# Twelve blocks of tokens in place of thirteen, in a gated scan followed by two MLPs on one core

## The chip, the core and the metric

The kernel runs on one core of a Trainium2 chip. TensorE (PE in the profile) does the matrix products, VectorE (DVE) and ScalarE (ACT) the elementwise work, SyncE (SP) issues most DMAs. The metric is the time of the device in microseconds, lower is better. A run of the kernel before takes 1091.85 us (median of three, 1091.34 to 1092.14).

## The reference

There are 6080 tokens of 256 channels. A gated scan runs along the tokens, channel by channel, and its output goes through two MLPs with 2048 hidden units each, one after the other:

```python
sig = 1.0 / (1.0 + np.exp(-f_logit))
f = lower_bound + (1.0 - lower_bound) * sig
i = 1.0 - f
for t in range(S):
    h = f[:, t] * h + i[:, t] * x[:, t]
    y[:, t] = h

h = y @ w_in_1                                  # 256 -> 2048
y1 = (h * sigmoid(1.702 * h)) @ w_out_1         # 2048 -> 256
h = y1 @ w_in_2
g = where(h >= 1, h, where(h <= -1, 0, (h + 1) ** 2 / 4))
out = g @ w_out_2
```

Inputs, `lower_bound` and the output are float32, the four weight matrices float64.

## The kernel before, in words

Channels and hidden units lie on the 128 partitions, tokens along the free axis. `token_blocks` cuts the 6080 tokens, 190 units of 32, into the fewest blocks of at most `MAXN` tokens, as even as units allow, the longer ones first. With `MAXN = 480` these are 8 blocks of 480 and then 5 of 448. A block goes through layer one and later through layer two.

A float32 operand of a product is split into a high and a low part of type float32r, and a product takes three matmuls: high by high, high by low, low by high (`three`, lines 298 to 300). A step is two tiles of 128 hidden units of one block in one layer: `up` makes the hidden values (two halves of the channels, two tiles, three passes: 12 matmuls), the activation follows on ScalarE and VectorE, `high` and `low` split it, and `down`, two steps later, adds the product with the output weights to the block's result (12 matmuls). A block takes 8 steps in each layer. A matmul has 128 x 128 stationary weights, and as many columns as the block has tokens; the weights change with every matmul.

The order of the steps: the first three blocks go through layer one together, by turns; then block 3; from then on layer two of block b and layer one of block b + 4 take turns, eight steps each (`LEAD = 4`). In that time the results of layer one wait in SBUF: `keep` copies a block's result from PSUM into the tile `ring{b % LEAD}`, one half on ScalarE (line 399), the other on VectorE (line 400), and `split_y1` reads it a step or two before layer two of the block begins (lines 431 and 432), and writes the high and the low part.

The weights are 32 units, each the input or the output weights of two tiles of hidden units. A unit comes in as the 64 bits of float64 (512 KB, `load_unit`), is taken apart and put together by integer operations, and ends as two resident tiles, high and low (`weight_high`, line 139, on ScalarE; `weight_low`, line 143, on VectorE). The first units are staged in the places of `ring0` to `ring2`, the later ones in `x0`. The last unit, the output weights of hidden tiles 14 and 15 in layer two, is put together in step 39.

The first three blocks are loaded by rows and turned on TensorE (`load_rows`, line 163; `turn_rows`, line 170), a quarter of the block on the partitions at a time. The sigmoid of block 2's forget rows is line 195, the conversions to gate and scan input lines 201 to 214, the scan line 259, the split of its output lines 277 and 283. The rows of x of block 2, the turned x of block 2 and the high part of block 3's scan output are one after the other in the place `ring3`. Later blocks are loaded in 32 x 32 blocks and turned on VectorE.

The order on the engines is written out by hand for the start and from step 40 on; for steps 5 to 39 a planner orders the instructions by its own costs. Tiles with the same tag share places, and an instruction that writes a tile waits until the readers of the tile that had the place before are done. SP issues DMAs in the order of the program, each behind such waits.

The end: in the last step the work goes by halves, `store_half` turns each half of the result on VectorE (line 417), and its DMAs go out by three queues.

Of the kernel before, what the change touches and what calls it, by code (L numbers as in the profile page):

```python
# [8 lines left out]
F32 = mybir.dt.float32  # L9
F32R = mybir.dt.float32r  # L10
# [4 lines left out]
P = 128  # L15
Q = 32
MAXN = 480
TOGETHER = 3
LEAD = 4


def token_blocks(n_tokens):
    """Even blocks of at most MAXN tokens, multiples of 32, the longer ones first."""
    units = n_tokens // Q
    assert units * Q == n_tokens
    count = -(-units // (MAXN // Q))
    out, t0 = [], 0
    for i in range(count):
        n = Q * (units // count + (i < units % count))
        out.append((t0, n))  # L30
        t0 += n
    return out
# [3 lines left out]
def tile_gated_scan_two_mlps(  # L36
# [10 lines left out]
):  # L47
    """Gated scan, then two MLPs, all with channels on partitions and tokens along the free axis.

    A float32 operand of a product is the exact sum of two float32r parts of 12 significant bits,  # L50
    high and low; a product takes three passes: high*high, high*low and low*high.

    The weights arrive as the 64 bits of a float64. The exponent field, the sign and the fraction
    are taken apart by integer operations and put together as a float32, rounded once.
    """
    nc = tc.nc
    NT, D = out.shape
# [25 lines left out]

# [1 line left out]
    w_in = (w_in_1, w_in_2)  # L85
    w_out = (w_out_1, w_out_2)
    weights = {}
    for layer in range(2):
        for kind in "io":
            for j in range(NP):  # L90
                weights[kind, layer, j] = tuple(
                    const.tile([P, 2, D], F32R, name=f"w{kind}{layer}_{j}{part}") for part in "hl"
                )
    units = [(kind, layer, j) for layer in range(2) for j in range(NP) for kind in "io"]
# [14 lines left out]
    def take_apart(i):  # L109
        """Exponent field, moved from the bias of a float64 to that of a float32, at least 0; 1 + high fraction."""  # L110
        words = staged[i]
        exponent = pool.tile([P, UW], U32, tag="c1", bufs=3, name=f"exponent{i}")
        fraction = pool.tile([P, UW], U32, tag="c2", name=f"fraction{i}")
        nc.vector.tensor_scalar(
            exponent, words[:, :, 1], 20, 0x7FF, ALU.logical_shift_right, ALU.bitwise_and
        )
        nc.vector.tensor_scalar(fraction, words[:, :, 1], 0xFFFFF, None, ALU.bitwise_and)
        nc.scalar.activation(exponent, exponent, AF.Relu, bias=rebias, scale=float(2**23))
        nc.scalar.activation(fraction.bitcast(F32), fraction, AF.Identity, bias=1.0, scale=2.0**-20)
        fields[i] = exponent, fraction.bitcast(F32)  # L120
# [16 lines left out]

    def weight_high(i):
        nc.scalar.copy(weights[units[i]][0].rearrange("p k c -> p (k c)"), joined[i])

# [3 lines left out]

# [1 line left out]
    # With r = 1 - sigmoid, the forget gate is 1 - (1 - lower_bound) * r and the input  # L146
    # (1 - lower_bound) * r * x.
    raw = {}
# [24 lines left out]
    def blocked(ap, b, q):  # L173
        """Channels q*32.. of each half, 32 tokens on partitions, for the transpose of 32x32."""
        t0, n = blocks[b]
        return ap[t0 : t0 + n, :].rearrange("(j i) (g q c) -> q i g j c", i=Q, g=ND, q=P // Q)[q]
# [20 lines left out]
    def start_gate(b, g, tag, bufs):  # L197
        """The gate of half a block from PSUM; its sigmoid is taken here or was taken before."""
        t = pool.tile([P, blocks[b][1]], F32, tag=tag, bufs=bufs, name=f"gate{b}_{g}")
        if b < 2:  # L200
            nc.scalar.activation(t, turned.pop(("f", b, g)), AF.Sigmoid, scale=-1.0)
        else:
            nc.scalar.copy(t, turned.pop(("f", b, g)))
        gates[b, g] = t
# [14 lines left out]
    def gate_half(b, g):  # L219
        """The same from tiles in blocks of 32 tokens; the results take the tiles' places."""  # L220
        n = blocks[b][1]
        f, xs = raw["f", b][:, g], raw["x", b][:, g]
        gate = pool.tile([P, n], F32, tag="c1", bufs=3, name=f"gate{b}_{g}")
        xt = pool.tile([P, n], F32, tag="c2", name=f"xt{b}_{g}")
        nc.vector.transpose(out=gate, in_=f)
        nc.vector.transpose(out=xt, in_=xs)
        nc.scalar.activation(f, gate, AF.Identity, scale=lb_minus_one[:, g : g + 1], bias=1.0)
        nc.vector.scalar_tensor_tensor(
            xs, gate, one_minus_lb[:, g : g + 1], xt, ALU.mult, ALU.mult
        )  # L230
        forgets[b, g] = f
        states[b, g] = xs
# [32 lines left out]
    def first_part(b, part):  # L265
        n = blocks[b][1]
        tag, bufs = f"x{b % 2 if b < 2 else (b + 1) % 2}", 2
        if b == 2:
            tag = "y1"
        if b == 3:  # L270
            tag, bufs = {"h": "ring3", "l": "r"}[part], 1
        return pool.tile([P, ND, n], F32R, tag=tag, bufs=bufs, name=f"x{b}{part}")
# [11 lines left out]

# [1 line left out]
    rounds = [(0, b, r - b // 2) for r in range(NP + 1) for b in range(TOGETHER)]  # L286
# [53 lines left out]
    def clamp(s, us):  # L340
        """c = min(max((h + 1) / 2, 0), 1) and r = max(h - 1, 0): the value is c * c + r."""
        n = tokens(s)
# [53 lines left out]
    def keep(b, y):  # L396
        n = blocks[b][1]
        t = pool.tile([P, ND, n], F32, tag=f"ring{b % LEAD}", bufs=1, name=f"ring{b}")
        nc.scalar.copy(t[:, 0], y[0][:, :n])
# [33 lines left out]

# [1 line left out]
    along = {}  # L435
# [18 lines left out]

    # the step in which a unit of weights is put together, one after it is taken apart
    put_at = {}
# [8 lines left out]
    late = [put_in[s] for s in range(22, n_steps) if s in put_in]  # L465
    # the first five units are put together before the regular steps
    for k, i in enumerate(early):
# [26 lines left out]

# [1 line left out]
    nc.scalar.preload_act_table(AF.Sigmoid)  # L496
# [29 lines left out]

    # the first units and the gates of the first blocks, by turns, so that the products start early
    take_apart(0)
# [17 lines left out]
    load_rows("f", 2, 0, rows("r", 1, "f", 2))  # L546
    x2 = pool.tile([P, ND, 4, P], F32, tag="ring3", bufs=1, name="rows_x2")
    for g in range(ND):
# [46 lines left out]
    start_gate(2, 1, "o", 1)  # L595
    x2t = pool.tile([P, ND, blocks[2][1]], F32, tag="ring3", bufs=1, name="turned_x2")
    start_input(2, 0, x2t[:, 0])
# [111 lines left out]
```

## Time and profile before

| what | value |
|---|---|
| time, median of 3 runs | 1091.85 us |
| span of the profiled execution, first to last instruction | 1089.4 us |
| TensorE, matmuls busy | 1073.8 us (99%) |
| TensorE, weight loads busy | 943.5 us (87%) |
| VectorE busy | 633.0 us (58%) |
| ScalarE busy | 727.5 us (67%) |
| matmuls and transposes on TensorE | 5040 |
| DMA bytes | 36.26 MB |

The profile is of one more execution. Of its own time it gives the span, 1089.4 us; the median of the runs is 2.45 us longer, and that lies outside the first and the last instruction. Weight loads (PEld) run beside matmuls. Matmuls are pipelined, and the ends that the profile shows for them are modelled, so the row of a matmul is longer than the step from its start to the next start.

### The profile page before, as it was taken

What the parts mean: (1) busy time and instruction counts of PE and PEld (TensorE: products, weight loads), DVE (VectorE), ACT (ScalarE), POOL (GpSimd) and SP (SyncE); (2) the same over time, 40 slices, a digit from 0 to 9 for tenths busy, and PEclk for the clock granted to TensorE, in tenths of its full rate; (3) what the DMA queues carried; (4) which work ended last, traced back from release to release, by engine and by line L of the source; (5) the groups of instructions that cost most, each with busy time, mean ns of one, the idle gap of its engine ahead of it and who ended that gap; (6) DMA issues with size and microseconds to landing.
All of it is one profiled execution on the core that took longest, in us unless ns stands there. A gap on an engine that the chain in (4) does not pass through costs nothing.

```text
span 1089.4 us, 12630 instructions
## 1 busy us (share of the span) xinstructions
PE 1073.8 (99%) x5040; PEld 943.5 (87%) x5040; DVE 633.0 (58%) x810; ACT 727.5 (67%) x842; POOL 2.8 (0%) x9
## 2 busy tenths in 40 slices
PE   6999999999999999999999999999999999999997
PEld 4788888888888888888889889889889999999996
DVE  6979959843743742752652652752752742566564
ACT  6877777956755755765665765765765754677775
POOL 0000000000000000000000000000000000000000
PEclk9999999999999999999999999999999999999999
DMA  8523241020021021011012012011011010010111
GB/s 205 117 97 114 91 81 64 34 41 15 1 37 19 1 33 22 1 23 31 1 17 36 1 19 34 1 23 30 1 26 27 1 17 1 1 17 2 17 17 17
DMA packets 138926, 36.26 MB, mean 33 GB/s; under 512 B 124884, under 2 KB 130644, under 8 KB 138868
## 3 DMA queue, kind: packets, MB, share of 16 engines
q1 hardware_dynamic: 137844, 35.24, 15.6%
q8 instruction: 39, 0.64, 0.2%
q0 software_dynamic: 96, 0.12, 0.1%
q10 hardware_dynamic: 928, 0.11, 0.1%
q14 instruction: 19, 0.16, 0.1%
HBM read 29.23 MB, written 6.23 MB: 33 GB/s over the span
## 4 chain that ended last, share of the span: by engine, by line
PE 95%; DMA 1%; DVE 1%; ACT 1%; SPq 1%; issue 0%; POOL 0%; POOLq 0%; ACTq 0%
PE y L300 16%; PE y L299 16%; PE h L300 16%; PE y L298 16%; PE h L298 16%; PE h L299 16%; DMA rows_f_o<-in_f_logit 1%; DMA rows_f_gh<-in_f_logit 1%; SPq L163 1%; DVE gl L367 0%; ACT gh L363 0%; DVE turned_x L259 0%; ACT g L337 0%; DVE turned_x L214 0%; ACT L337 0%
## 5 line engine op out<-in xcount | busy, mean ns | idle before, releaser
L367 DVE TENSOR_TENSOR gl<-g,gh 128x960 fp32r<-128x960 f32 (+2 forms) x209 | 235.5, 1127 | 284.1 <-ACT gh L363 284.0
L363 ACT CAST gh<-g 128x960 fp32r<-128x960 f32 (+2 forms) x209 | 202.4, 969 | 122.0 <-PE y L300 107.9
L347 ACT ACTIVATE g<-h,half 128x960 f32<-128x960 f32 (+2 forms) x105 | 108.7, 1035 | 130.3 <-PE h L300 126.7
L337 ACT ACTIVATE g<-h 128x960 f32<-128x960 f32 (+1 forms) x104 | 98.9, 952 | 74.6 <-PE h L300 74.4
L354 DVE TENSOR_TENSOR g<-g,r 128x960 f32<-128x960 f32 (+2 forms) x105 | 117.2, 1117 | 10.8 <-ACT g L353 10.7
L349 DVE TENSOR_SCALAR g<-g 128x960 f32<-128x960 f32 (+2 forms) x105 | 67.2, 640 | 73.9 <-ACT g L347 73.6
L348 ACT ACTIVATE r<-h,minus_one 128x960 f32<-128x960 f32 (+2 forms) x105 | 108.0, 1029 | 0.0
L353 ACT ACTIVATE g<-g 128x960 f32<-128x960 f32 (+2 forms) x105 | 103.2, 984 | 0.0
L299 PE MATMUL y<-gl,wo_6h 128*128 128x480 f32 (+1 forms) x104 | 39.0, 375 | 0.6 <-DVE gl L367 0.6
L300 PE MATMUL y<-gh,wo_1l 128*128 128x480 f32 (+1 forms) x104 | 39.1, 376 | 0.1
L299 PE MATMUL y<-gl,wo_1h 128*128 128x480 f32 (+1 forms) x104 | 39.0, 375 | 0.0
L300 PE MATMUL y<-gh,wo_5l 128*128 128x480 f32 (+1 forms) x104 | 39.0, 375 | 0.0
L300 PE MATMUL y<-gh,wo_0l 128*128 128x480 f32 (+1 forms) x104 | 39.0, 375 | 0.0
L300 PE MATMUL y<-gh,wo_2l 128*128 128x480 f32 (+1 forms) x104 | 39.0, 375 | 0.0
L300 PE MATMUL y<-gh,wo_4l 128*128 128x480 f32 (+1 forms) x104 | 39.0, 375 | 0.0
L298 PE MATMUL y<-gh,wo_1h 128*128 128x480 f32 (+1 forms) x104 | 39.0, 377 | 0.0
L300 PE MATMUL y<-gh,wo_7l 128*128 128x480 f32 (+1 forms) x104 | 39.0, 375 | 0.0
L300 PE MATMUL y<-gh,wo_6l 128*128 128x480 f32 (+1 forms) x104 | 39.0, 375 | 0.0
L298 PE MATMUL y<-gh,wo_4h 128*128 128x480 f32 (+1 forms) x104 | 39.0, 375 | 0.0
L298 PE MATMUL y<-gh,wo_5h 128*128 128x480 f32 (+1 forms) x104 | 39.0, 375 | 0.0
L298 PE MATMUL y<-gh,wo_2h 128*128 128x480 f32 (+1 forms) x104 | 39.0, 375 | 0.0
L298 PE MATMUL y<-gh,wo_3h 128*128 128x480 f32 (+1 forms) x104 | 39.0, 375 | 0.0
(1434 smaller groups left out, 2688.4 us busy)
## 6 DMA issues: line engine op xcount, KB each, us to landing
stage<-in_moe_w_in SPq DMA_DIRECT2D x16, 512.0 KB, 3.6
stage<-in_moe_w_out SPq DMA_DIRECT2D x16, 512.0 KB, 3.4
out_y<-o SPq DMA_DIRECT2D x32, 120.0 KB, 3.1
raw_f<-in_f_logit SPq DMA_DIRECT2D x20, 120.0 KB, 3.5
raw_x<-in_x SPq DMA_DIRECT2D x20, 120.0 KB, 3.7
raw_f<-in_f_logit SPq DMA_DIRECT2D x20, 112.0 KB, 3.2
raw_x<-in_x SPq DMA_DIRECT2D x20, 112.0 KB, 3.2
out_y<-o SPq DMA_DIRECT2D x16, 112.0 KB, 2.9
```

The lines of the kernel that those rows point to most:

```text
L163: nc.sync.dma_start(out=t, in_=src.rearrange("(c p) d -> p c d", p=m))
L298: nc.tensor.matmul(ps, lhsT=wh, rhs=mh, start=first, stop=False)
L299: nc.tensor.matmul(ps, lhsT=wh, rhs=ml, start=False, stop=False)
L300: nc.tensor.matmul(ps, lhsT=wl, rhs=mh, start=False, stop=last)
L337: nc.scalar.activation(g, hidden.pop(s)[:, :, :n], AF.Gelu_apprx_sigmoid)
L347: nc.scalar.activation(g, ps, AF.Relu, scale=0.5, bias=half)
L348: nc.scalar.activation(r, ps, AF.Relu, bias=minus_one)
L349: nc.vector.tensor_scalar(g, g, 1.0, None, ALU.min)
L353: nc.scalar.activation(g, g, AF.Square)
L354: nc.vector.tensor_tensor(g, g, r, ALU.add)
L363: nc.scalar.copy(parts[s][0][:, us], act[s][:, us])
L367: nc.vector.tensor_tensor(l[:, us], act[s][:, us], h[:, us].bitcast(F32), ALU.subtract)
```

## The change

`MAXN` becomes 512, so that `token_blocks` gives 12 blocks: 10 of 512 tokens and then 2 of 480. The tiles that are as long as a block or as `MAXN` grow with it. The results of layer one are kept in three places, `ring{b % 3}`, in place of four. The place `ring3` is renamed `late`, and after the high part of block 3's scan output it takes both parts of the last weight unit, which had a resident tile for each part before; the tile is made when the unit is put together. The rest of the diff removes comments. Its core:

```diff
-MAXN = 480
+MAXN = 512
 TOGETHER = 3
 LEAD = 4
+RING = 3
...
     for layer in range(2):
         for kind in "io":
             for j in range(NP):
-                weights[kind, layer, j] = tuple(
-                    const.tile([P, 2, D], F32R, name=f"w{kind}{layer}_{j}{part}") for part in "hl"
-                )
+                if (kind, layer, j) != ("o", 1, NP - 1):
+                    weights[kind, layer, j] = tuple(
+                        const.tile([P, 2, D], F32R, name=f"w{kind}{layer}_{j}{part}") for part in "hl"
+                    )
...
     def weight_high(i):
+        if units[i] not in weights:
+
+            t = pool.tile([P, 2, 2, D], F32R, tag="late", bufs=1, name="wo_last")
+            weights[units[i]] = t[:, 0], t[:, 1]
         nc.scalar.copy(weights[units[i]][0].rearrange("p k c -> p (k c)"), joined[i])
...
         if b == 3:
-            tag, bufs = {"h": "ring3", "l": "r"}[part], 1
+            tag, bufs = {"h": "late", "l": "r"}[part], 1
...
     def keep(b, y):
         n = blocks[b][1]
-        t = pool.tile([P, ND, n], F32, tag=f"ring{b % LEAD}", bufs=1, name=f"ring{b}")
+        t = pool.tile([P, ND, n], F32, tag=f"ring{b % RING}", bufs=1, name=f"ring{b}")
...
-    x2 = pool.tile([P, ND, 4, P], F32, tag="ring3", bufs=1, name="rows_x2")
+    x2 = pool.tile([P, ND, 4, P], F32, tag="late", bufs=1, name="rows_x2")
...
-    x2t = pool.tile([P, ND, blocks[2][1]], F32, tag="ring3", bufs=1, name="turned_x2")
+    x2t = pool.tile([P, ND, blocks[2][1]], F32, tag="late", bufs=1, name="turned_x2")
```

## Rows read from the trace of the kernel before

**Rows 1.** The page, part 1: span; engine, busy us (share) and instructions.
```profile
span 1089.4 us, 12630 instructions
...
PE 1073.8 (99%) x5040; PEld 943.5 (87%) x5040; DVE 633.0 (58%) x810; ACT 727.5 (67%) x842; POOL 2.8 (0%) x9
```

**Rows 2.** The page, part 2: granted clock of TensorE in 40 slices, in tenths.
```profile
PEclk9999999999999999999999999999999999999999
```

**Rows 3.** Waits of PE: line, releaser, us in total, times, longest; first and last of eight.
```profile
PE turned L170 <- DMA rows_f_r<-in_f_logit: 5.7, 1, 5.7
...
PE h L299 <- DVE x2l L283: 0.2, 1, 0.2
```

**Rows 4.** Windows: stretch, length, busy us (count) by engine, granted clock, DMA share, GB/s.
```profile
core 0: us, PE busy (x) PEld busy (x) DVE busy (x) ACT busy (x) POOL busy (x), PEclk, DMA share, GB/s
200.30:554.81 354.51, 354.51 (x1633) 306.25 (x1632) 186.33 (x214) 230.94 (x251) 0.00 (x0) 1.00 0.11 17
817.96:1063.29 245.33, 245.33 (x1201) 225.30 (x1200) 130.12 (x147) 166.44 (x187) 0.00 (x0) 1.00 0.07 11
0.00:22.00 22.00, 14.07 (x58) 10.04 (x58) 14.16 (x29) 11.31 (x19) 1.55 (x7) 1.00 0.94 228
22.00:42.00 20.00, 18.43 (x80) 13.91 (x81) 18.57 (x31) 17.88 (x27) 0.00 (x0) 1.00 0.36 100
80.00:100.00 20.00, 20.00 (x93) 17.27 (x93) 20.00 (x34) 15.74 (x22) 0.00 (x0) 1.00 0.37 126
```

**Rows 5.** Timeline of PE inside one step of 480 columns: start, us, what.
```profile
304.57 0.37 PE L298 MATMUL h<-y_1h,wi_7h 128*128 128x480 f32 x1
304.78 0.38 PE L299 MATMUL h<-y_1l,wi_7h 128*128 128x480 f32 x1
...
305.45 0.37 PE L299 MATMUL h<-y_1l,wi_7h 128*128 128x480 f32 x1
```

**Rows 6.** DMA issues: tile, queue, operation, count, KB each, us from issue to landing.
```profile
rows_f_o<-in_f_logit SPq DMA_DIRECT2D x1, 240.0 KB, 8.1
```

**Rows 7.** The chain that ended last, first and last of its pieces from 21.89 to 41.63.
```profile
21.89 0.63 ACT rows_f_o L195
...
41.63 0.48 PE y L300
```

**Rows 8.** Groups by line and shape, ScalarE and VectorE: count | busy us, mean ns | idle before.
```profile
L363 ACT CAST gh<-g 128x960 fp32r<-128x960 f32 x128 | 127.1, 993 | 67.5 <-PE y L300 55.2 <-DVE g L354 6.3 <-PE h L300 5.8
L363 ACT CAST gh<-g 128x896 fp32r<-128x896 f32 x79 | 74.2, 939 | 54.2 <-PE y L300 52.7 <-PE h L300 1.4
...
L367 DVE TENSOR_TENSOR gl<-g,gh 128x960 fp32r<-128x960 f32 x128 | 148.0, 1156 | 152.8 <-ACT gh L363 152.8
L367 DVE TENSOR_TENSOR gl<-g,gh 128x896 fp32r<-128x896 f32 x79 | 86.3, 1093 | 131.2 <-ACT gh L363 131.2
...
L259 DVE TENSOR_TENSOR_SCAN raw_x<-forget,carry,raw_x 128x448 f32<-128x448 f32 x10 | 11.4, 1144 | 0.0
...
L259 DVE TENSOR_TENSOR_SCAN raw_x<-forget,carry,raw_x 128x480 f32<-128x480 f32 x6 | 7.3, 1208 | 0.0
```

**Rows 9.** Timeline of the end: PE, then the output.
```profile
1078.94 0.47 PE L299 MATMUL y<-gl,wo_6h 128*128 128x448 f32 x1 [0.56 <-DVE gl L367]
...
1083.51 0.37 PE L300 MATMUL y<-gh,wo_7l 128*128 128x448 f32 x1
...
1084.60 0.94 ACTq L419 DMA_DIRECT2D out_y<-o  x2
```

**Rows 10.** Timeline around the copies into the ring and the last weight unit.
```profile
181.82 0.38 PE L300 MATMUL h<-x3h,wi_7l 128*128 128x480 f32 x1
...
183.08 1.15 DVE L432 TENSOR_TENSOR y_0l<-ring,y_0h 128x960 fp32r<-128x960 f32 x1
...
194.87 0.55 ACT L399 COPY ring<-y 128x480 f32<-128x480 f32 x1
...
212.00 0.61 ACT L139 CAST wo_7h<-exponent 128x512 fp32r<-128x512 f32 x1
```

## The prediction

> **What bounds the kernel now.** I read the page first: of a span of 1089.4 us TensorE's matmul row is busy for 1073.8 [rows 1], and its granted clock shows as 9 (90% or more) in all 40 slices [rows 2], 1.00 in the windows of below: the 2.4 GHz level. A busy matmul row alone doesn't prove a bound, so the waits of PE come next. There are eight, 5.7 us the longest and 0.2 the shortest, and all belong to the start or to the last two steps [rows 3]; from 42 us to 1078 us no matmul waits for another engine. The reader is to see there that vector, scalar and DMA work are hidden in that stretch, so that only two things can move the time: how long one matmul takes from its start to the start of the next (the spacing), times their number, and the two ends of the program.
>
> The view by windows gives the spacing [rows 4]. From 200.30 to 554.81 us all blocks have 480 tokens: 354.51 us hold 1632 matmuls (the view counts one more, which the window's edge cuts), so 217.22 ns each, and 24 of them, one step, 5.213 us. From 817.96 to 1063.29 us all blocks have 448: 245.33 us, 1200 matmuls, 204.44 ns, 4.907 us a step. The same rows give the load of the stationary weights, 306.25 us for 1632 and 225.30 us for 1200, which is 187.7 ns in both: a load doesn't depend on the block, and lies beside the matmul.
>
> **The change part by part.** *Blocks.* 6080 tokens are 190 units of 32. At most 15 in a block gave 13 blocks, 8 of 480 and 5 of 448; at most 16 give 12, 10 of 512 and 2 of 480. A block costs 8 steps in each layer, a step 24 matmuls. Before: 8 x 384 = 3072 matmuls of 480 columns and 5 x 384 = 1920 of 448. After: 3840 of 512 and 768 of 480. The columns stay the same; 384 matmuls, with their weight loads, go.
>
> Before, by the two spacings: 3072 x 217.22 ns = 667.3 us and 1920 x 204.44 ns = 392.5 us, together 1059.8 us. The spacing at 512 columns is not in the trace. The line through the two rows has 12.78 ns per 32 columns, 0.399 ns a column, and gives 230.0 ns. At 2.4 GHz a tick is 0.417 ns; that the two widths differ by nearly one tick a column says that a matmul takes a tick for each column and a fixed part, which is 217.2 - 200.0 = 17.2 ns at 480 and 17.8 at 448. At 448 the ticks (186.7 ns) are no longer than the weight load (187.7), which could make that row a little dear; with the fixed part of 480 the spacing at 512 is 213.3 + 17.2 = 230.6 ns. I take 230.3, between these. The bounds, from the spacings inside one step at 480 [rows 5]: the start at 304.57 is followed by the next after 0.21 us, and the three spacings from 304.78 to 305.45 take 0.67 us, 223 ns each. As fixed parts these are 10 and 23 ns, and would make 223 to 237 ns at 512. I take the middle because the step as a whole comes back in every step of the stretch with the same mean, and a single position in it does not.
>
> After: 3840 x 230.3 ns = 884.4 us and 768 x 217.22 ns = 166.8 us, together 1051.2 us. The steady part is **8.6 us** shorter; its bounds are 35 us shorter (223 ns) and 17 us longer (237 ns).
>
> The rule for this spacing in the Trainium skill ("TensorE: Matmul & The Clock Gate", section "Back-to-back issue gap") is N/2.4 plus about 2.5 ns. It would give 202.5 ns at 480 where the row has 217.2, so the fixed part is some 15 ns larger here, and the measurement decides. If only 2.5 ns went with each of the 384 matmuls, the steady part would lose 1.0 us in place of 8.6, which speaks against the change.
>
> *Start.* The blocks loaded by rows grow from 240 to 256 KB a transfer. When the last one that holds something up, the forget rows of block 2, lands (issued at 13.74 us, 8.1 us later [rows 6]), 12 such transfers and 3 weight units have been moved; 12 x 16 KB more at the 228 GB/s of the first 22 us [rows 4] is 0.86 us. From its sigmoid at 21.89 to the last stall of a matmul at 41.63 us the chain runs over ScalarE and VectorE [rows 7]; 14 of its pieces are as wide as a block, the others (weights of 512, a table load) stay. The slopes come from the pairs of widths [rows 8]: a ScalarE cast 993 against 939 ns for 64 columns, so 54 for a pair of tiles and 27 for one; a VectorE subtraction 1156 against 1093, so 63 and 32; a scan 1208 against 1144 for 32. Four wide and two narrow on ScalarE, two wide and four narrow on VectorE and two scans make 0.27 + 0.25 + 0.13 = 0.65 us. So the last stall ends 1.5 us later. But by then some 89 matmuls of the layers have run (the two windows up to 42 us show 138 on PE, of which 48 are transposes and one is counted in both), and each has done 13.1 ns more of work, 1.17 us. Net loss at the start **0.35 us**. Bounds: -1.2, if the loads and the chain don't grow at all, and 2.8, if all of the first 41.6 us grow by 6.7% and nothing is absorbed.
>
> *End.* The last block has 480 tokens in place of 448. The chain of its last step (to the stall at 1078.94 [rows 9]) and the matmuls beside it grow alike. Behind the last matmul at 1083.51 stand one transpose and an output that end at 1089.4; of these 5.9 us a fifteenth, 0.4 us, is the most, nothing the least. The transpose and the packets alone grow, not the latency: **0.15 us**.
>
> *Ring of three.* The copy of a block's output into the ring now also waits for the split of the output three blocks earlier. That split of block 0 ends on VectorE at 184.23 us, and the copy of block 3 starts at 194.87 [rows 10]: 10.6 us of cover, two steps. For later blocks there are three steps between them in the code. So nothing. Were the cover gone, the copy would hold up what is queued behind it on ScalarE, the cast of a step, and the matmuls would follow a step later. *The shared tile* takes the last output unit after the high half of block 3 has been read. Its last reader starts at 181.82 us, the cast that writes the unit at 212.00 [rows 10], 30 us later: nothing again. If the cast did come late, it would hold ScalarE. The row tiles of block 2 only change the name of their place. One block's set of small instructions (table loads, split, ring copies, stores) disappears from engines that nobody waits for: nothing.
>
> Sum: -8.6 + 0.35 + 0.15 = -8.1 us. The sum is made against the span of 1089.4, which becomes 1081.3; the median of the runs, 1091.85, is 2.45 us above the span, and I leave that as it is: **1083.7 us**.
>
> **The rivals.**
> *The spacing goes with the columns.* If most of the 17 ns is no price per matmul but slower streaming (0.4525 ns a column, 217.22/480), 512 take 231.7 ns, the steady part is 889.7 + 166.8 = 1056.5, 3.3 us less than before, and with 0.5 at the ends the time is 1089.0. Against it: 448 would take 202.8, and has 204.4; but the line hangs on two widths that are close together. The Trainium skill's gap rule of above, with its 2.5 ns, is the far end of this rival; it would leave 1091.3.
>
> *The full width costs more than it saves.* At 512 columns a tile's halves lie exactly 2048 bytes apart and a matmul fills its place in PSUM to the end. If a matmul then disturbs its neighbours or the readers of that place in most positions as the worst do now, the spacing is 237 ns [rows 5], 3840 x 6.7 ns = 25.7 us more than I forecast: 1109.4. This decides from 230.3 + 8.1/3.84 = 232.4 ns on, only 2.1 ns away. For it: the spacing inside a step varies by more than that. Against it: the mean of the fixed part moved by 0.6 ns between 448 and 480, though their places in memory differ too.
>
> *Another order at the start.* Steps 5 to 39 are ordered by the planner, whose costs change with the widths. VectorE is busy for all of 20 us in 80 to 100 us [rows 4], so a worse order could make matmuls wait. One step lost (5.5 us) gives 1089.2. Against it: its weight work stays the same while each step gets 0.3 us longer, so its share falls.
>
> *A smaller fixed part.* At 10 ns [rows 5] the steady part loses 35 us: 1057. Only for it: such positions occur.
>
> **How the numbers follow.** The forecast 0.66, with 1081 to 1087 as its own range (230.0 to 230.6 ns, and the ends from -0.7 to +2.5); the spacing by columns 0.12; the dear full width 0.10; the order 0.08; the small fixed part 0.04. Of these, 1079.0 to 1090.5 holds the forecast, the spacing by columns and most of the order's cases. A measurement of this kernel can tell about 0.2% from no change, 2.2 us: faster is under 1089.7. The forecast, the small part, two thirds of the columns' case and a third of the order's make 0.81; the rest of these two 0.09; the dear width 0.10.
>
> **What would show it.** Right: 4608 matmuls of the layers beside 48 transposes, 230 ns in a window of 512, 217.2 still at 480, weight loads of 187.7 ns; no wait of PE between 45 us and the last step; the last stall at the start near 43 us; the copies into the ring idle for nothing. Wrong: a spacing over 232.4 ns at 512 (the gain is gone), one of 231.7 (it goes by columns), or waits of PE between 45 and 250 us (the order).

## The result and the profile after

The changed kernel takes **1067.61 us** (median of four runs, 1067.00 to 1068.23) against 1091.59 us for the kernel before (four runs, 1089.52 to 1092.14): a ratio of 0.9783, 95% interval 0.9769 to 0.9797. The forecast was 1083.7 with a range from 1079.0 to 1090.5. The direction was right, the size was not: 24 us came where 8 were forecast. The profiled execution has a span of 1065.2 us, 24.2 less than before.

The page of the changed kernel, part 1 and one row of part 2, read as [rows 1, 2]:

```profile
span 1065.2 us, 11693 instructions
...
PE 1049.5 (99%) x4656; PEld 871.0 (82%) x4656; DVE 626.1 (59%) x762; ACT 717.1 (67%) x785; POOL 2.9 (0%) x9
...
PEclk9999999999999999999999999999999999999999
```

There are 4656 matmuls and transposes, 384 fewer, as the working had it; the granted clock is at its 2.4 GHz level in every slice in both kernels, so the clock explains nothing. PE's waits are of the kind in [rows 3], but for one: the last line of the shown ones, a wait of 0.3 us for ScalarE at 56.58 us, lies among the planned steps, where the profile names none in the kernel before. From 61 us to the last two steps it names none here either:

```profile
PE turned L176 <- DMA rows_f_r<-in_f_logit: 5.7, 1, 5.7
PE turned L176 <- ACT rows_f_r L201: 1.3, 1, 1.3
...
PE y L305 <- DVE gl L373: 0.6, 1, 0.6
...
PE h L304 <- ACT g L343: 0.3, 1, 0.3
...
```

```profile
56.58 0.50 PE L304 MATMUL h<-x2h,wi_1h 128*128 128x512 f32 x1 [0.33 <-ACT g L343]
```

The windows decide, as in [rows 4]. The second last line is a stretch of 80 steps of 512 columns, the last one of 11 steps of 480 (columns: stretch, length, busy time and count by engine, clock, DMA share, GB/s):

```profile
core 0: us, PE busy (x) PEld busy (x) DVE busy (x) ACT busy (x) POOL busy (x), PEclk, DMA share, GB/s
...
6.00:12.00 6.00, 5.86 (x27) 4.51 (x26) 5.30 (x10) 4.04 (x8) 0.00 (x0) 1.00 1.16 306
...
304.73:740.00 435.27, 435.27 (x1922) 360.55 (x1921) 225.15 (x240) 280.27 (x286) 0.00 (x0) 1.00 0.12 19
985.80:1042.93 57.13, 57.13 (x266) 49.50 (x264) 33.97 (x36) 42.74 (x46) 0.00 (x0) 1.00 0.12 18
```

The same stretch of 512 columns cut exactly at the first matmul of a step on both sides, PE alone:

```profile
304.73:739.93 435.20, 435.20 (x1922) 1.00 0.12 19
```

435.20 us for 80 x 24 = 1920 matmuls (the edges cut two more) is **226.67 ns** a matmul, where I had taken 230.3. At 2.4 GHz that is 544 ticks: one for each of the 512 columns and exactly 32 more. At 480, 57.13 us for 264 matmuls is 216.4 ns, against 217.22 in [rows 4]. The weight load is 360.55/1921 = 187.7 ns, as before. Inside a step of 512 nothing varies any more, where [rows 5] had 210 and 223 ns side by side (start, length, what):

```profile
304.73 0.39 PE L304 MATMUL h<-y_1h,wi_5h 128*128 128x512 f32 x1
304.95 0.39 PE L305 MATMUL h<-y_1l,wi_5h 128*128 128x512 f32 x1
305.18 0.39 PE L306 MATMUL h<-y_1h,wi_5l 128*128 128x512 f32 x1
305.41 0.39 PE L304 MATMUL h<-y_1h,wi_5h 128*128 128x512 f32 x1
```

**Where the 24 us came from.** Write every spacing as (columns + 32) ticks and an excess. Before: 3072 x 213.33 + 1920 x 200.00 ns = 1039.4 us, and the measured 1059.8 has 20.5 us of excess on that, 3.9 ns a matmul at 480 and 4.4 at 448. After: 3840 x 226.67 + 768 x 213.33 ns = 1034.2 us, measured 3840 x 226.67 + 768 x 216.4 = 1036.6, so 2.4 us of excess. In this account, which takes N + 32 ticks (N for the columns) as the price of every matmul, the 384 matmuls that went were worth 5.1 us (384 x 13.33 ns), and the other 18.1 us are excess that the matmuls of 512 don't have. The ends (span less this steady part) went from 29.6 to 28.6 us.

At the start the rows of block 2 land sooner than in [rows 6], though they are larger (tile, queue, KB, us from issue to landing):

```profile
rows_f_o<-in_f_logit SPq DMA_DIRECT2D x1, 256.0 KB, 5.7
```

The first matmul of the layers starts at 12.70 us (15.33 before) and the last stall of the start ends at 40.45 us (41.63 before [rows 7]):

```profile
12.70 0.48 PE L304 MATMUL h<-x0h,wi_0h 128*128 128x512 f32 x1
```

```profile
40.45 0.50 PE L306 MATMUL y<-gh,wo_1l 128*128 128x512 f32 x1
```

The ring and the shared tile, to be held against [rows 10]; nothing in brackets behind a line means that it waited for nobody:

```profile
186.78 1.22 DVE L438 TENSOR_TENSOR y_0l<-ring,y_0h 128x1024 fp32r<-128x1024 f32 x1
```

```profile
201.68 0.58 ACT L405 COPY ring<-y 128x512 f32<-128x512 f32 x1
```

```profile
214.62 0.61 ACT L145 CAST wo_last<-exponent 128x512 fp32r<-128x512 f32 x1
```

The split ends at 188.0 us, the copy that has to wait for it starts 13.7 us later; the cast of the last unit comes 27 us behind the start of the last reader of its place (187.51). The end, against [rows 9]: the last matmul at 1059.14, its output at 1060.27, and 6.06 us from that matmul to the end of the span (5.9 before).

```profile
1059.14 0.37 PE L306 MATMUL y<-gh,wo_last 128*128 128x480 f32 x1
...
1060.27 0.95 ACTq L425 DMA_DIRECT2D out_y<-o  x2
```

So the question for the experiments: why does a matmul of 512 columns cost 3.6 ns less than I had taken from 448 and 480, and why has it no excess? Where a kernel below was run once, its time is compared with runs of the kernel before on the same chip, 1089.9 to 1093.2 us in all; its own verdict rests on the spacing, which its windows give to 0.1 ns.

### The profile page after: what moved, and what is told of

It reads as the page before. It is cut to its first block, busy times and chain, and to the rows that moved or that the text cites. A ratio compares the mean times of both kernels' runs of the same rounds, so it can differ in the third digit from the quotient of the medians.

```text
span 1065.2 us, 11693 instructions
## 1 busy us (share of the span) xinstructions
PE 1049.5 (99%) x4656; PEld 871.0 (82%) x4656; DVE 626.1 (59%) x762; ACT 717.1 (67%) x785; POOL 2.9 (0%) x9
## 4 chain that ended last, share of the span: by engine, by line
PE 94%; DVE 3%; ACT 2%; DMA 0%; issue 0%; SPq 0%; POOL 0%; POOLq 0%; ACTq 0%; DVEq 0%
PE h L304 16%; PE y L305 16%; PE h L305 16%; PE y L306 16%; PE h L306 16%; PE y L304 16%; DVE gl L373 1%; DMA rows_x_o<-in_x 0%; ACT g L343 0%; DVE state L265 0%; ACT gh L369 0%; ACT L343 0%; DVE turned_x L265 0%; ACT exponent L120 0%; DVE fraction L130 0%
## 5 line engine op out<-in xcount | busy, mean ns | idle before, releaser
L373 DVE TENSOR_TENSOR gl<-g,gh 128x1024 fp32r<-128x1024 f32 (+2 forms) x193 | 233.0, 1208 | 274.5 <-ACT gh L369 274.3
L369 ACT CAST gh<-g 128x1024 fp32r<-128x1024 f32 (+2 forms) x193 | 199.4, 1034 | 119.6 <-PE y L306 102.3
L353 ACT ACTIVATE g<-h,half 128x1024 f32<-128x1024 f32 (+2 forms) x97 | 106.6, 1099 | 120.7 <-PE h L306 120.7
L343 ACT ACTIVATE g<-h 128x1024 f32<-128x1024 f32 (+1 forms) x96 | 97.6, 1017 | 72.3 <-PE h L306 65.8
L360 DVE TENSOR_TENSOR g<-g,r 128x1024 f32<-128x1024 f32 (+2 forms) x97 | 116.1, 1198 | 13.6 <-ACT g L359 13.5
L354 ACT ACTIVATE r<-h,minus_one 128x1024 f32<-128x1024 f32 (+2 forms) x97 | 106.1, 1094 | 0.0
L355 DVE TENSOR_SCALAR g<-g 128x1024 f32<-128x1024 f32 (+2 forms) x97 | 66.0, 680 | 66.8 <-ACT g L353 66.6
L359 ACT ACTIVATE g<-g 128x1024 f32<-128x1024 f32 (+2 forms) x97 | 101.7, 1049 | 0.2 <-DVE g L355 0.2
L305 PE MATMUL y<-gl,wo_6h 128*128 128x512 f32 (+1 forms) x96 | 37.3, 389 | 0.6 <-DVE gl L373 0.6
L306 PE MATMUL y<-gh,wo_1l 128*128 128x512 f32 (+1 forms) x96 | 37.3, 389 | 0.1
```

The source lines that it names most:

```text
L305: nc.tensor.matmul(ps, lhsT=wh, rhs=ml, start=False, stop=False)
L306: nc.tensor.matmul(ps, lhsT=wl, rhs=mh, start=False, stop=last)
L343: nc.scalar.activation(g, hidden.pop(s)[:, :, :n], AF.Gelu_apprx_sigmoid)
L353: nc.scalar.activation(g, ps, AF.Relu, scale=0.5, bias=half)
L354: nc.scalar.activation(r, ps, AF.Relu, bias=minus_one)
L355: nc.vector.tensor_scalar(g, g, 1.0, None, ALU.min)
```

## The experiments

### 1. All widths in one kernel

The changed kernel with the blocks written out, six of 512 and then each width down to 288.

```diff
-    count = -(-units // (MAXN // Q))
...
+    for u in [16, 16, 16, 16, 16, 16, 15, 14, 13, 12, 11, 10, 9, 10]:
+        out.append((t0, Q * u))
+        t0 += Q * u
```

> The changed kernel with fourteen blocks of 512 (six), 480, 448, 416, 384, 352, 320, 288 and 320 tokens, so that one run shows the spacing of matmuls at eight widths. At 512 the trace of the changed kernel has 226.67 ns, which is N + 32 ticks of 2.4 GHz, in every position of a step. Theory A, the weight load sets the pace below: the price is N + 32 ticks (512: 226.7, 480: 213.3, 448: 200.0, 416: 186.7, 384: 173.3) wherever that leaves room for a load of 187 to 188 ns and its hand-over, and a floor of about 200 to 205 ns below; so 480 a little over 213 (216 to 217), 448 204, and 416, 384 and narrower all stay near 200 to 205. Theory B, 512 is a special width (tiles 2048 bytes apart, the place in PSUM full) and all others pay about 17 ns: 416 190 to 191, 384 177, 352 164, 320 150. Theory C, the spacing goes by columns, 0.4427 ns each: 416 184, 320 142.

Measured: 1077.82 us. PE's windows, each of four steps (96 matmuls) of one width, from 480 down to 288:

```profile
424.94:445.71 20.77, 20.77 (x98) 1.00 0.18 28
509.38:528.83 19.45, 19.45 (x97) 1.00 0.20 31
591.17:609.19 18.02, 18.02 (x97) 1.00 0.22 35
670.18:686.82 16.64, 16.64 (x98) 1.00 0.25 39
744.52:759.91 15.39, 15.39 (x98) 1.00 0.26 40
813.55:827.63 14.08, 14.08 (x98) 1.00 0.27 42
877.10:889.79 12.69, 12.69 (x98) 1.00 0.32 49
```

| columns | 512 | 480 | 448 | 416 | 384 | 352 | 320 | 288 |
|---|---|---|---|---|---|---|---|---|
| measured, ns | 226.67 | 216.4 | 202.6 | 187.7 | 173.3 | 160.3 | 146.7 | 132.2 |
| columns + 32 ticks, ns | 226.67 | 213.33 | 200.0 | 186.67 | 173.33 | 160.0 | 146.67 | 133.33 |
| excess, ns | 0 | 3.0 | 2.6 | 1.0 | 0 | 0.3 | 0 | -1.1 |

None of the expected outcomes came. There is no floor by the weight load: the spacing falls to 132 ns with loads that still take 187 to 188 ns, so loads overlap each other, and a load's row is a latency, not a pace. Two loads among matmuls of 288 columns (start, length, what):

```profile
880.28 0.19 PEld L302 LDWEIGHTS h<-x12l,wi_4h 128*128 128x128 f32 x1
880.41 0.19 PEld L303 LDWEIGHTS h<-x12h,wi_4l 128*128 128x128 f32 x1
```

512 is not special either: 384 and 320 have the same 32 ticks. And the time doesn't go by columns at 0.4427 ns each, which would be 184 ns at 416 and 142 at 320. N + 32 ticks is what 512, 384 and 320 take; 480, 448 and 416, two of which I had drawn my line through, lie above it, and 288 lies 1.1 ns below, so that N + 32 ticks is no least price either.

### 2. Shorter weight loads

The kernel before, with the second pass and, but for the last of a sum, the third on 64 of the 128 stationary columns (the other half of these products is left out).

```diff
-        nc.tensor.matmul(ps, lhsT=wh, rhs=ml, start=False, stop=False)
-        nc.tensor.matmul(ps, lhsT=wl, rhs=mh, start=False, stop=last)
+        nc.tensor.matmul(ps[:64], lhsT=wh[:, :64], rhs=ml, start=False, stop=False)
+        if last:
+            nc.tensor.matmul(ps, lhsT=wl, rhs=mh, start=False, stop=True)
+        else:
+            nc.tensor.matmul(ps[:64], lhsT=wl[:, :64], rhs=mh, start=False, stop=False)
```

> The kernel before, with 64 in place of 128 stationary columns in the second and third pass of a product (but the last of a sum), so half of what these passes add is left out; two thirds of the weight loads of the second half of a step and half of those of the first half become shorter, the moving columns stay. Theory A (the load's pace): a load of 64 columns takes about half of 187.7 ns, and the positions behind it fall to N + 32 ticks: the second half of a step at 480 from a mean of 218.9 to 213 to 215 ns, at 448 from 203.2 to 200 to 201.5; the span becomes 8 to 18 us shorter. Theory B (512 is a special width): no position changes by more than 1 ns, the span stays within 2 us of 1089.4.

Measured: 1086.41 us. Windows of 2232 matmuls of 480 and of 1224 of 448:

```profile
70.64:553.80 483.16, 483.16 (x2233) 1.00 0.17 38
815.36:1063.56 248.20, 248.20 (x1226) 1.00 0.07 11
```

216.5 ns in place of 217.22, and 202.8 in place of 204.44, though the short loads last 133 to 138 ns and not 187.7. The span is 4.8 us shorter than that of the kernel before, between what the two theories wanted. Shorter loads take away a part of the excess (0.7 of 3.9 ns, 1.7 of 4.4) and not all of it. The edit also halves the output that these passes write, so that this part needn't be the loads' own.

### 3. The ring and the shared tile alone

The changed kernel with blocks of at most 480 again: only the ring of three and the shared tile are left of the change.

```diff
-MAXN = 512
+MAXN = 480
```

> The change without its blocks: MAXN stays 480 (thirteen blocks), the ring of three and the shared tile of the last weight unit are in. My account (ring and shared tile cost and bring nothing, the covers are 10.6 and 30 us): within 0.2% of the kernel before, 1089.5 to 1093.8, spacing 217.2 ns at 480 and 204.4 at 448. The rival, that the order or the places made by them give part of the 24 us: 1088 or less.

Measured: 1091.26 us (ten runs, 1090.17 to 1091.72) against 1091.51; ratio 0.9998, interval 0.9988 to 1.0007. The spacings are those of [rows 4]: 485.00 us for 2232 matmuls is 217.3 ns, 250.24 for 1224 is 204.44.

```profile
68.89:553.89 485.00, 485.00 (x2233) 1.00 0.17 37
817.04:1067.28 250.24, 250.24 (x1226) 1.00 0.07 10
```

Ring and shared tile cost nothing and bring nothing that ten runs can tell. They make room for the tiles of 512, and the gain comes with the blocks.

### 4. Eleven blocks of 512 and one of 448

```diff
-    count = -(-units // (MAXN // Q))
...
+    for u in [16, 16, 16, 16, 16, 16, 16, 16, 16, 16, 16, 14]:
+        out.append((t0, Q * u))
+        t0 += Q * u
```

> The changed kernel with eleven blocks of 512 and one of 448 in place of ten of 512 and two of 480. By the spacings 4224 x 226.67 + 384 x 204.4 ns = 1036.0 us against 3840 x 226.67 + 768 x 216.4 ns = 1036.6, and a shorter last block: 1066.5 to 1067.3, 0.3 to 1 us less than the changed kernel's 1067.6. If 448 as the last block makes the end shorter by as much as the fifteenth of 5.9 us, 1066.3. If wider blocks were worth more than their spacing says (theory: a fixed loss per block change), 1065 or less.

Measured: **1066.34 us** (four runs, 1065.75 to 1066.61) against 1091.51 before; ratio 0.977, interval 0.9754 to 0.9787. Of all versions it has the lowest median, and its slowest run is under the fastest of the change; but the intervals of the two ratios overlap, so that it is ahead, by 0.1%, is not settled. The time is a little under the 1066.5 to 1067.3 expected. By the spacings it should be ahead: 4224 x 226.67 + 384 x 202.6 ns = 1035.3 us against 1036.6.

### 5. Short blocks in wide places

The changed kernel with thirteen blocks of 480 and 448 again, and every streamed tile laid out as if its block had 512.

```diff
-    count = -(-units // (MAXN // Q))
+    count = -(-units // 15)
...
-        return pool.tile([P, ND, n], F32R, tag=tag, bufs=bufs, name=f"x{b}{part}")
+        return pool.tile([P, ND, MAXN], F32R, tag=tag, bufs=bufs, name=f"x{b}{part}")[:, :, :n]
...
-            pool.tile([P, ND, n], F32R, tag=tag, name=f"y1_{b}{part}") for part in "hl"
+            pool.tile([P, ND, MAXN], F32R, tag=tag, name=f"y1_{b}{part}")[:, :, :n] for part in "hl"
```

> The changed kernel with thirteen blocks of at most 480 as before, but every tile that a product streams (both splits of the inputs and the split of the activation) laid out for 512, so that the halves lie 2048 bytes apart. Widths as before, places as after. Theory W (the excess over N + 32 ticks belongs to the widths 480 and 448): spacing 216 to 218 ns at 480 and 202 to 205 at 448, time 1087 to 1092. Theory P (it belongs to the places, and 2048 bytes apart heals it): 213.3 ns at 480 and 200.0 at 448, so 3072 x 3.9 + 1920 x 4.4 ns = 20 us less, 1071 to 1074.

Measured: 1093.99 us (ten runs, 1093.00 to 1095.06) against 1091.20; ratio 1.0028, interval 1.0018 to 1.0038. 2232 matmuls of 480 and 1224 of 448:

```profile
69.93:553.75 483.82, 483.82 (x2234) 1.00 0.17 38
817.80:1070.76 252.96, 252.96 (x1226) 1.00 0.07 10
```

216.8 ns at 480, a little better; 206.7 at 448, worse by 2.2. That and the time are above what either theory allowed. So the places move a spacing, in both directions, but halves 2048 bytes apart don't take the excess from 480 and 448. That this distance alone explains the gain has fallen. The places are not quite those of the change: the tile `o` has 3840 bytes here in place of 4096, so that the streamed tiles behind it begin 256 bytes nearer to the weights. In experiment 9 such a distance changes nothing at 512, nor at 480 (216.4 ns); at 448 it was not tried.

### 6. Wide blocks in uneven places

The changed kernel with the halves of the tiles `gh` and `gl` 2112 bytes apart in place of 2048, which also shifts the tiles behind them.

```diff
-                pool.tile([P, 2, MAXN], F32R, tag=f"g{part}", name=f"g{part}{s}")[:, :, :n]
+                pool.tile([P, 2, MAXN + 16], F32R, tag=f"g{part}", name=f"g{part}{s}")[:, :, :n]
```

> The changed kernel with the halves of the split activation 2112 bytes apart in place of 2048; blocks of 512 stay. The first twelve matmuls of a step stream other tiles and are the control. Theory W: the second half of a step at 512 stays at 226.67 ns, the time within 2 us of 1067. Theory P: the second half rises to 229 to 231, the first stays, 1840 x 2 x 3 ns make 6 to 9 us more.

Measured: 1082.53 us, some 15 us above the change. 3000 matmuls of 512:

```profile
71.05:763.59 692.54, 692.54 (x3002) 1.00 0.16 32
```

230.8 ns, 4.2 above N + 32 ticks. With 64 bytes more between the halves of `gh` and `gl` the changed kernel becomes almost the one I forecast (230.3 ns, 1083.7 us). At 512, then, places decide.

But the control failed: not only the second half of a step rose. Its first half, which streams other tiles, did too. In the trace the first halves have a mean of 230.0 ns and the second halves 231.6; one step, by the first matmul of each half and of the next step:

```profile
320.39 0.40 PE L304 MATMUL h<-y_1h,wi_7h 128*128 128x512 f32 x1
323.15 0.40 PE L304 MATMUL y<-gh,wo_5h 128*128 128x512 f32 x1
325.92 0.39 PE L304 MATMUL h<-x5h,wi_0h 128*128 128x512 f32 x1
```

That is 230 ns for the first twelve and 231 for the other twelve. The first half's own tiles lie as in the change modulo 256 bytes: the two places of `gh` and the two of `gl` are 128 bytes longer each, and what lies behind all four moves by 512. Yet its spacings run from 226 to 236 ns by position and come back to 226.6 to 227.0 only in the last two of the twelve. So a disturbed half seems to carry over into the next one; how is not shown.

### 7. Everything moved by 32 bytes

The kernel before, with 32 bytes ahead of all tiles.

```diff
+    const.tile([P, 8], F32, name="pad")
     lb = const.tile([P, ND], F32, name="lb")
```

> The kernel before with a tile of 32 bytes put ahead of all others, so that weights and activations begin at a multiple of 128 bytes and not at 96 beyond one; nothing else changes. Theory W: 217.2 and 204.4 ns stay within 0.3, time within 2 us of 1091.5. Theory P in the form that the absolute place counts: the spacings fall toward 213.3 and 200.0, up to 20 us less, or move by over 1 ns either way.

Measured: 1089.28 us, and the spacings of [rows 4] unchanged (484.97 us for 2232 matmuls is 217.28 ns; 250.24 for 1224, 204.44):

```profile
68.53:553.50 484.97, 484.97 (x2233) 1.00 0.16 37
816.65:1066.89 250.24, 250.24 (x1225) 1.00 0.06 10
```

Moving all tiles by 32 bytes changes no spacing; the time is 2.2 us under the 1091.5 that it was to stay within 2 us of. The step of block 1 with `wi_3` starts at 63.3 us here, at 63.7 in experiment 3 and at 64.6 in the kernel before, though all three have the same work there: the start varies by over 1 us between executions.

### 8. Two blocks of 480 first

```diff
+    for u in [15, 15, 16, 16, 16, 16, 16, 16, 16, 16, 16, 16]:
+        out.append((t0, Q * u))
+        t0 += Q * u
```

> The changed kernel with its two blocks of 480 first and not last: the blocks 0 and 1 are loaded over 120 partitions in place of 128, block 2 over 128. Theory S (the start gained since transfers over 128 partitions are faster: 306 GB/s in 6 to 12 us against 248, and landing in 5.3 to 5.8 us against 6.1 to 7.1): the first layer matmul starts near 15.3 us as before in place of 12.7, and the time is 1.0 to 2.5 us longer than the changed kernel's 1067.6: 1068.6 to 1070.1. Rival (the start gained from other things, and shorter first blocks shorten the chain): first layer matmul at 12.3 to 12.9 us, time 1066.8 to 1067.9.

Measured: 1067.94 us (four runs, 1067.61 to 1068.64); ratio 0.9789, interval 0.9775 to 0.9804, no different from the change; the start came near theory S, the time to the rival's upper edge. Its window from 6 to 12 us, to be held against the 306 GB/s of the change:

```profile
6.00:12.00 6.00, 5.45 (x23) 3.91 (x24) 4.79 (x10) 3.59 (x7) 0.00 (x0) 1.00 1.12 262
```

The kernel before has 248 GB/s in this stretch. A quarter of a block lies on 120 partitions there (240 KB a transfer) and on 128 in the change (256 KB), and the transfers over 128 go faster: in this stretch the eight kernels that begin with blocks of 512 have 289 to 309 GB/s, the six that begin with 480 have 230 to 262. That part is shown. The first matmul of the layers then starts at 14.60 us here and at 12.70 in the change, but the first one with output weights, in step 2, starts at 30.20 us in both. What the faster loads are worth in the end is not shown.

### 9 to 12. The distance between the weights and the streamed tiles

The changed kernel with an unused tile between the weights and the streamed tiles, of 256, 64 and 128 bytes; and, in the last, 128 bytes ahead of all tiles, so that weights and streamed tiles move together. The four differ in size and place of one line:

```diff
                     weights[kind, layer, j] = tuple(
                         const.tile([P, 2, D], F32R, name=f"w{kind}{layer}_{j}{part}") for part in "hl"
                     )
+    const.tile([P, 64], F32, name="pad")
```

> The changed kernel with 256 bytes between the weights and all tiles that are streamed; the streamed tiles keep their distances (all starts equal modulo 2048), only their place against the weights moves, from 0 to 256 bytes modulo 2048. Theory R (what counts is the place of the streamed tile against the weights that load beside it): the exact N + 32 ticks at 512 are lost, spacing 228 to 232 ns, 1072 to 1088 us. Theory U (it is enough that streamed tiles lie alike): 226.67 ns stay, 1066.5 to 1068.5 us; then the excess of the run with halves 2112 bytes apart came from unlike distances alone.

> The same with 64 bytes between weights and streamed tiles. Theory R: spacing at 512 between 227 and 232 ns, 1068.5 to 1088 us, another value than with 256. Theory U: 226.67 ns, 1066.5 to 1068.5 us.

> The changed kernel with 128 bytes between weights and streamed tiles; 64 gave 228.8 ns at 512, 256 gave the exact 226.67. In the kernel before, every second half of a tile at 480 begins 128 bytes off modulo 256. Theory R128 (the place counts modulo 128): 226.67 ns, 1066.5 to 1068.5 us; then the halves of the kernel before were no worse placed for being 128 off, and its excess at 480 hangs on the width. Theory R256 (modulo 256): 228 to 231 ns, 1071 to 1084 us.

> The changed kernel with 128 bytes ahead of all tiles, so that weights and streamed tiles move together: the streamed tiles begin where they began in the run that took 1088.9 us (128 bytes between weights and streamed tiles), but lie against the weights as in the changed kernel. Theory relative (the place of the streamed tile against the weights counts): 226.67 ns at 512, 1066 to 1069 us. Theory absolute (the streamed tile's own place modulo 256 counts): 231 to 233 ns, 1085 to 1091 us.

Windows of 125 steps, 3000 matmuls of 512 each; first 256 bytes, 1068.46 us:

```profile
71.91:752.28 680.37, 680.37 (x3001) 1.00 0.16 32
```

64 bytes, 1077.59 us:

```profile
72.36:759.03 686.67, 686.67 (x3002) 1.00 0.16 32
```

128 bytes, 1088.91 us, against 1091.76 for the kernel before on that chip:

```profile
71.49:768.39 696.90, 696.90 (x3001) 1.00 0.15 31
```

128 bytes ahead of everything, 1068.06 us:

```profile
71.40:751.82 680.42, 680.42 (x3002) 1.00 0.16 32
```

| streamed tiles against weights | spacing at 512 | time |
|---|---|---|
| as in the change | 226.67 ns | 1067.6 us |
| 64 bytes further | 228.9 ns | 1077.6 us |
| 128 bytes further | 232.3 ns | 1088.9 us |
| 256 bytes further | 226.8 ns | 1068.5 us |
| both 128 bytes further | 226.8 ns | 1068.1 us |

These windows begin earlier than that of the change and hold the stall near 160 us; over the same steps the change has 226.7 ns. The run with 256 bytes came out as theory U had it, the one with 64 as R, and the last as "relative". The one with 128 speaks for R256, but was dearer than its range (228 to 231 ns, 1071 to 1084 us).

That is the clearest result of the study, each line of it from one run. An unused tile of 128 bytes a partition takes 21 of the 24 us back, with no wait of PE between 62 us and the last two steps; 256 bytes do nothing, and 128 do nothing when the weights move along. At 512 columns the place of the streamed tiles relative to the weights decides, and the four distances fit a period of 256 bytes. The pad moves the tiles of the other engines too, so their work could have collided with the weights instead; but in the run with 128 bytes the matmuls beside which neither ScalarE nor VectorE is busy (229 of them, from 200 to 750 us) have 232.1 ns as well.

In the change every half of a tile is 2048 bytes in blocks of 512, eight times 256, and so all of them begin alike; in the kernel before a half was 1920 bytes at 480, 7.5 times 256, so that second halves lay 128 bytes off. It doesn't follow that this is the excess of the kernel before: experiment 5 has no such halves, and 216.8 ns. Nor do 480 columns answer to the 128 bytes as 512 do. Eleven steps of 480 of the run with 128 bytes take 216.5 ns a matmul, where the change has 216.4:

```profile
1007.65:1064.80 57.15, 57.15 (x266) 1.00 0.12 18
```

## Why the prediction was wrong, point by point

**What bounds the kernel: right.** From 61 us to the last two steps the profile names no wait of TensorE, in both kernels; only spacing times number, and the ends, moved the time.

**Blocks and counts: right.** 3840 and 768 matmuls, 384 fewer, and loads of 187.7 ns that lie beside the matmuls.

**The step that failed is the spacing at 512**: "a matmul takes a tick for each column and a fixed part, which is 217.2 - 200.0 = 17.2 ns at 480", carried over to 512 as 230.6, and 230.3 taken. The mechanism (a tick a column and a fixed part) held and the fixed part was mis-sized: in the layout of the change it is 32 ticks, 13.33 ns, at 512, and experiment 1 has it at 384 and 320 too. What 480 and 448 carry above it, 3.9 and 4.4 ns, can't be carried over to 512; it hangs on the width, and at 448 on the places too (202.6 to 206.7 ns), and its cause stays open. In this account a matmul that went was worth 13.3 ns and not 17.2, but each of the 3840 of 512 columns took 3.6 ns less than forecast, 13.9 us. With 0.6 us of the blocks of 480 (216.4 for 217.22) and 1.5 at the ends this is the 16.1 us between a span 8.1 shorter and one 24.2 shorter.

Two rows ahead of the result spoke for it. The slope of 0.399 ns a column lies below a tick, 0.417, so the "fixed" part was larger at 448 than at 480, which no fixed part can be; I explained that away by the weight load, and experiment 1 shows spacings far below the load. And [rows 5] have spacings from 210 to 223 ns in one step, where the steps of 512 don't vary. I bounded with them, and then took the middle.

The rule that I weighed, N/2.4 plus about 2.5 ns (the Trainium skill, "TensorE: Matmul & The Clock Gate", section "Back-to-back issue gap"), was right in its form and not in its size here: by it I estimate 215.8 ns at 512, and the trace has 226.67. The page gives it for a single matmul's gap, and for a stream with loads a figure of its own, about 131 ns at 512, which no run here comes near. Of the loads the same page says (section "Step-by-step: what each phase is for") that the weights have a read port of their own, so that loading the next ones takes no read bandwidth from the matmul that runs. Experiments 9 to 12 don't agree in full: where weights and streamed tiles lie relative to each other is worth up to 5.6 ns a matmul at 512. Which access is in the other's way they don't show.

**Start: the sign was wrong.** I had 0.35 us lost, and the last stall near 43 us; it came at 40.45, 1.2 us sooner than before. With the work that is done by then, 88 matmuls that each took 9.5 ns more (0.8 us), the start gained 2.0 us in the terms of the sum, beyond the bound of -1.2. I had let transfers grow at the 228 GB/s of before; with 128 partitions they run at 306 GB/s in the stretch from 6 to 12 us. That this gave the 2.0 us is not shown: the start varies by over 1 us between executions (experiments 3 and 7).

**End: right**, 0.16 us where I had 0.15. **Ring and shared tile: right**, nothing (experiment 3). **Order at the start:** the steps 5 to 39 lost about 1.1 us in three stalls (0.63, 0.29 and 0.18 us, near 56, 60 and 160 us) where before they lost 0.4, so 0.7 us. The sum had nothing for this. The first of them is a wait between 45 and 250 us, the sign that I had named for the rival of the order; but its lost step of 5.5 us didn't come.

**The rivals.** The spacing by columns has fallen at the width that it was about: 512 take 226.67 ns and not 231.7. The widths from 480 down to 288 would not have decided that; they lie within 2 ns of 0.4525 ns a column. The smaller fixed part, at 10 ns, was the nearest to what came, with the wrong size (13.3); its reason, positions inside a step that lie closer, was the right row to read: its 210 ns are near the 213.3 that N + 32 ticks gives. The dear full width is the most instructive. Its reason, halves 2048 bytes apart and a full place in PSUM, did no harm: the change has both, and no excess. But a price of that order exists on this chip for another layout: with 128 bytes between weights and streamed tiles 512 columns take 232.3 ns, against the limit of 232.4 that I had given, and the same edit was worth 3 us there. The range was too narrow because I had taken a width's spacing for a property of the width alone.

**What stays open.** Why the period is 256 bytes, if it is one (192 bytes and distances over 256 were not tried), and which access it is that collides. Why 480, 448 and 416 carry 1 to 4 ns in most layouts. Why 448 takes 206.7 ns in wide places and 202.6 in experiment 1: in both all streamed tiles lie at multiples of 256 bytes from the weights, so that the place modulo 256 can't be the whole rule at this width. Why 288 is 1.1 ns below N + 32 ticks. And how the excess of one half of a step reaches the next (experiment 6). Thirteen blocks were tried with no other distance of the halves than 2048 bytes (experiment 5).

## What to carry to other kernels

On a kernel that TensorE bounds, take the spacing of matmuls from more than two widths, or at least test it: a slope below a tick a column, or spacings that vary inside a step without a wait, say that something besides the columns is in it. Before counting on a gain from another tile size, list where the streamed tiles and the weights will lie modulo 256 bytes; here, with blocks of 512, a layout 128 bytes off cost 21 us of 1068, and it shows in no wait of the steady part, in no granted clock, and hardly in TensorE's busy share (99% in both). Blocks of 512 with one short remainder are worth a try beside even blocks: eleven of 512 and one of 448 ran at 1066.3 us, which isn't settled to be ahead.

## What the runs showed of the hardware

With weights that change at every matmul, float32r, at the 2.4 GHz level: a spacing of N + 32 ticks at 512, 384 and 320 columns (226.67, 173.3, 146.7 ns) in the layout of the change, and more at 416 (1.0 ns), 448 (2.6 to 6.7) and 480 (3.0 to 3.9).

The distance between streamed tiles and weights changes that spacing at 512: 226.67 ns as in the change, 228.9 with 64 bytes more, 232.3 with 128, 226.8 with 256. At 480 the 128 bytes do nothing (216.5 ns for 216.4).

Weight loads of 187 to 188 ns overlap: the matmuls with 288 columns follow one another every 132 ns. Loads of 64 columns take 133 to 138 ns; with them in most second and third passes the spacing at 480 is 0.7 ns shorter (experiment 2).

Transfers by rows over 128 partitions moved 306 GB/s in the stretch from 6 to 12 us (289 to 309 in eight kernels), over 120 partitions 248 (before) and 262 (experiment 8).
